# A decode step of cached attention plus a token mixer: mixer matmuls moved out of the last head, denominators before values, and more of the last V summed directly by [d, head]

## The chip, the cores and the metric

The kernel runs on one core of a Trainium2 chip. The metric is the device time of one execution, in microseconds (us), as the median of several executions. A profiled execution also gives a trace; its span is some 2 us shorter than the time (1274.7 against 1276.45 for the kernel before). Between traces, only durations and differences inside the span are compared.

In the profile, PE is TensorE's matmuls, PEld its weight loads, DVE is VectorE, ACT is ScalarE, and SP is the queue that issues the loads. The granted clock is the share of its full clock that the trace shows for TensorE; "half clock" is a stretch at 0.50. In a chain of waits, "issue" is time in which the engine waited for nothing that the profile shows.

## The reference

One query token attends over a cache of 65536 keys and values for 8 key-value heads (16 query heads, so 2 share each cache head; head size 256). K and V are 268 MB each in bf16. Beside it runs a small MLP ("mixer"), and a gate mixes both:

```
q = x @ wq                                  # 16 heads of 256
p = softmax(q . k * 256**-0.5)              # over 65536 positions
a = (p @ v) @ wo                            # 448 outputs
u = gelu(layernorm(x) outer w1 + b1)        # 448 x 1792
b = u @ w2 + b2                             # 448 outputs: "the mixer matmuls" do u @ w2
out = g * a + (1 - g) * b                   # g = sigmoid(x . gate_w)
```

## The kernel before

The cache comes in 32 rounds, 4 for each of 8 heads. A round is two K halves of 4 MB and one V buffer of 8 MB (128 tiles of 128 positions). For each round TensorE transposes K, makes the scores (`keys`), ScalarE takes exponentials into `pT`, and TensorE adds V into `acc` (`values`: two rows of 256, at four places of the partition axis, by `n % 4`) and the denominators through a matrix of ones. At a head's end `acc` is copied (`take`), turned into [d, head] by two products (`by_d`), divided by the denominators, and projected with `wo` (`project`).

The end of TensorE's program, and the `values` before (cuts marked):

```
pieces = [(0, 64), (64, 96), (96, 112), (112, 120), (120, 128)]   # the last V comes in five loads
NLATE = 112
...
def values(c0, n1=NV, last=False):
    for n in range(n1):
        r, nt = divmod(n, NT)
        if nt == 0 and r >= BODY - 2 and not last:
            pe.wait_ge(sem_exp, c0 + (r + 3))
        ...                                    # last: wait for the piece that n begins
        pe.matmul(acc[o:o + REP, 0:DH], pT[:, r, 2 * nt:2 * nt + 2], vbuf[:, n, :], ...)
    for r in range(BODY):                      # the 8 denominator matmuls
        ins = pe.matmul(acc[:, DENC:SELC], ones_sq[:, :], pT[:, r, :], ...)
    ins.then_inc(sem_pv, 1)                    # frees V; in the last round also starts `take`
...
# after the loop over heads and rounds:
pe.wait_ge(sem_exp, NC + 2)
pe.wait_ge(s_pb, FT)
for kt in range(FT):                           # FT = 14: the mixer matmuls
    ins = pe.matmul(sps[0:1, 1, 0:DM], w2p_b[:, kt:kt + 1], gu[:, kt, :], ...)
ins.then_inc(s_bmm, 1)
values(NC - BODY, n1=NLATE, last=True)
pe.wait_ge(s_cp, H)
by_d(sps[:, 0, 0:2 * REP], True)
for n in range(NLATE, NV):                     # tiles 112 to 127 straight by [d, head]
    ...
    for dj in range(2):
        ins = pe.matmul(sps[:, 0, dj * REP:(dj + 1) * REP], vbuf[:, n, dj:DH:2], pT[...], ...)
ins.then_inc(s_late, 1)
pe.wait_ge(sem_wo, 16 * H)
pe.wait_ge(s_oTn, H)
project()
```

The loads are issued in the order K half, K half, V. A K half is issued when the chunks of the half it replaces are transposed, a V when `sem_pv` says that the last one is used up. The "late tiles" are those that are summed directly by [d, head], two narrow matmuls for a tile, and need no copy behind them.

The softmax here doesn't subtract the row's maximum and nothing guards it: scores larger than these inputs give would overflow.

## Time and profile before

| | before |
|---|---|
| time, median of 3 | 1277.2 us (1276.92 to 1277.43) |
| load queue busy | 99.3% of 16 engines' span, 427 GB/s |
| TensorE / VectorE / ScalarE busy | 73% / 33% / 42% |
| end of the last key work | 1260.56 |
| last V piece landed | about 1267.3 |
| end of the last late tile | 1271.15 |
| end | 1274.7 |

First the page of the kernel before: part 3, the one large queue (packets, MB, share of the 16 DMA engines' span), and two lines of part 6 with the loads of the last V (size, us from issue to landing; the last line is the median of the last two pieces).

```profile
q1 hardware_dynamic: 16866, 544.22, 99.3%
...
vbuf<-in_A_v_cache_dram SPq DMA_DIRECT2D x1, 4096.0 KB, 23.6
...
vbuf<-in_A_v_cache_dram SPq DMA_DIRECT2D x2, 512.0 KB, 31.3
```

The loads never stop (99.3% of the 16 engines' span), so work taken out of the middle of the stream can save time only if the stream itself then gets faster. The five pieces were issued from 1233.79 to 1235.6; the last took 31.7 us and landed at about 1267.3.

Now the chain of waits, in order of time, at its end (start us, length us, what):

```profile
1258.96 1.59 PE sps L268 x64
1260.56 0.02 issue
1260.58 0.21 ACT pT L573
1260.79 0.52 issue
1261.31 3.65 PE sps L376 x12
...
1265.70 3.16 PE acc L292 x105
1268.86 0.31 PE acc L295 x8
...
1269.19 0.47 DVE accs L488
...
1269.70 0.64 PE sps L301 x4
1270.34 0.81 PE sps L388 x32
...
1271.48 0.93 PE prj L313 x4
```

L268 are the scores, L376 the mixer, L292 values, L295 denominators, L488 the copy, L301 `by_d`, L388 the late tiles, L313 the projection. There is no load in this stretch: after 1260.56 TensorE is never short of V, and its work ends the kernel. From the end of the key work to the end of the span it takes 14.1 us, and the mixer makes up about 4.4 of it.

### The profile page before, as it was taken

What the parts mean: (1) busy time and instruction counts of PE and PEld (TensorE: products, weight loads), DVE (VectorE), ACT (ScalarE), POOL (GpSimd) and SP (SyncE); (2) the same over time, 40 slices, a digit from 0 to 9 for tenths busy, and PEclk for the clock granted to TensorE, in tenths of its full rate; (3) what the DMA queues carried; (4) which work ended last, traced back from release to release, by engine and by line L of the source; (5) the groups of instructions that cost most, each with busy time, mean ns of one, the idle gap of its engine ahead of it and who ended that gap; (6) DMA issues with size and microseconds to landing.
All of it is one profiled execution on the core that took longest, in us unless ns stands there. A gap on an engine that the chain in (4) does not pass through costs nothing.

```text
span 1274.7 us, 37399 instructions
## 1 busy us (share of the span) xinstructions
PE 936.7 (73%) x16919; PEld 853.6 (67%) x16919; DVE 415.5 (33%) x727; ACT 534.9 (42%) x786; POOL 0.9 (0%) x7
## 2 busy tenths in 40 slices
PE   3878775878767687668876776866778667787768
PEld 3767765777657676567765676756677666777657
DVE  2786331333223332123331233312233222332223
ACT  1555433554324543335533345433455333553434
POOL 0000000000000000000000000000000000000000
PEclk9888888897778887788987789878889788898879
DMA  9999999999999999999999999999999999999996
GB/s 409 423 430 416 428 428 424 439 435 428 444 423 429 433 449 432 411 438 433 443 430 438 415 430 437 435 438 423 433 430 444 428 428 427 436 428 435 444 424 286
DMA packets 16892, 544.41 MB, mean 427 GB/s; under 512 B 1768, under 2 KB 3819, under 8 KB 4206
## 3 DMA queue, kind: packets, MB, share of 16 engines
q1 hardware_dynamic: 16866, 544.22, 99.3%
q8 instruction: 8, 0.13, 0.0%
q14 instruction: 6, 0.05, 0.0%
q10 hardware_dynamic: 12, 0.01, 0.0%
HBM read 544.22 MB, written 0.00 MB: 427 GB/s over the span
## 4 chain that ended last, share of the span: by engine, by line
DMA 75%; PE 20%; DVE 2%; issue 1%; ACT 1%; DVEq 0%; SPq 0%
DMA vbuf<-in_A_v_cache_dram 67%; PE acc L292 13%; DMA kring<-in_A_k_cache_dram 8%; PE kst L256 5%; PE sps L268 1%; PE acc L295 1%; ACT zring L569 0%; DVE ktT L483 0%; PE sps L376 0%; DVE zring L460 0%; DVE zring L464 0%; DVE wtmp L458 0%; DVE wtmp L454 0%; DVE uring L456 0%; PE prj L313 0%
## 5 line engine op out<-in xcount | busy, mean ns | idle before, releaser
L583 ACT ACTIVATE ktT<-kst 128x1024 bf16<-128x1024 bf16 x512 | 498.0, 1021 | 694.6 <-PE kst L256 694.3
L256 PE MATMUL kst<-ident,kring 128*128 128x128 f32 x4096 | 545.8, 293 | 125.3 <-DMA kring<-in_A_k_cache_dram 99.5
L483 DVE COPY ktT<-kst 128x1024 bf16<-128x1024 bf16 x512 | 352.8, 691 | 726.2 <-PE kst L256 703.8
L256 PEld LDWEIGHTS kst<-ident,kring 128*128 128x128 f32 x4096 | 494.5, 152 | 135.1 <-issue 115.8
L292 PE MATMUL acc<-vbuf,pT 128*2 128x256 bf16 x4080 | 179.3, 357 | 187.0 <-DMA vbuf<-in_A_v_cache_dram 186.2
L292 PEld LDWEIGHTS acc<-vbuf,pT 128*2 128x2 bf16 x4080 | 117.2, 108 | 242.1 <-DMA vbuf<-in_A_v_cache_dram 188.8
L268 PEld LDWEIGHTS sps<-qcur,ktT 128*128 128x128 bf16 x8192 | 238.4, 96 | 6.6 <-DVE ktT L483 3.7
L268 PE MATMUL sps<-qcur,ktT 128*128 128x2 bf16 x8192 | 237.5, 164 | 3.6 <-DVE ktT L483 3.5
L573 ACT ACTIVATE pT<-sps 128x32 bf16<-128x32 f32 x256 | 52.2, 204 | 13.4 <-PE sps L268 13.4
L488 DVE COPY accs<-acc 128x288 f32<-128x288 f32 x8 | 3.7, 458 | 98.1 <-PE acc L295 98.1
L295 PEld LDWEIGHTS acc<-pT,ones_sq 128*128 128x128 bf16 x256 | 8.5, 96 | 7.2 <-issue 7.2
L295 PE MATMUL acc<-pT,ones_sq 128*128 128x32 bf16 x256 | 11.7, 178 | 0.0
L313 PE MATMUL prj<-wo_sb,oTn 128*1 128x448 bf16 x32 | 9.1, 417 | 3.2 <-DVE oTn L499 3.2
L569 ACT ACTIVATE zring<-zring 128x448 bf16<-128x448 bf16 x14 | 8.1, 577 | 6.7 <-DVE zring L466 6.6
L330 PE MATMUL acc<-ones_sq,gu 1*128 1x1 bf16 x42 | 1.3, 161 | 8.4 <-DMA b_b<-in_B_b_dram 8.4
L330 PEld LDWEIGHTS acc<-ones_sq,gu 1*128 1x128 bf16 x42 | 1.2, 99 | 8.5 <-DMA b_b<-in_B_b_dram 8.5
L313 PEld LDWEIGHTS prj<-wo_sb,oTn 128*1 128x1 bf16 x32 | 2.4, 87 | 5.9 <-issue 4.6
L476 DVE TENSOR_TENSOR gu<-wtmp,zring 128x448 bf16<-128x448 bf16 x14 | 5.5, 392 | 1.1
L460 DVE TENSOR_TENSOR zring<-wtmp,uring 128x448 bf16<-128x448 bf16 x14 | 5.5, 392 | 1.0
L458 DVE TENSOR_TENSOR wtmp<-uring 128x448 bf16<-128x448 bf16 x14 | 5.5, 392 | 1.0
L464 DVE TENSOR_TENSOR zring<-uring,wtmp 128x448 bf16<-128x448 bf16 x14 | 5.5, 392 | 1.0
L306 PE MATMUL acc<-zrow,ones_sq 1*128 1x292 bf16 x8 | 2.5, 312 | 3.9 <-DVE accs L488 3.9
(79 smaller groups left out, 78.2 us busy)
## 6 DMA issues: line engine op xcount, KB each, us to landing
kring<-in_A_k_cache_dram SPq DMA_DIRECT2D x64, 4096.0 KB, 27.8
vbuf<-in_A_v_cache_dram SPq DMA_DIRECT2D x1, 4096.0 KB, 23.6
wo_sb<-in_A_wo_dram SPq DMA_DIRECT2D x8, 448.0 KB, 31.4
vbuf<-in_A_wq_dram SPq DMA_DIRECT2D x1, 3072.0 KB, 10.1
vbuf<-in_A_v_cache_dram SPq DMA_DIRECT2D x1, 2048.0 KB, 28.1
vbuf<-in_A_v_cache_dram SPq DMA_DIRECT2D x1, 1024.0 KB, 30.1
vbuf<-in_A_v_cache_dram SPq DMA_DIRECT2D x2, 512.0 KB, 31.3
vbuf<-in_A_wq_dram SPq DMA_DIRECT2D x1, 512.0 KB, 10.8
```

The lines of the kernel that those rows point to most:

```text
L256: ins = pe.transpose(kst[:, b, j * P:(j + 1) * P], kring_f[:, a, r * NT + 4 * b + j, :], ident[:, :])
L268: ins = pe.matmul(sps[:, par, 2 * nt:2 * nt + 2], ktT[:, par, b, ntl * DH + dj:(ntl + 1) * DH:2], qcur[:, dj, :], start=(dj == 0), stop=(d ...
L292: pe.matmul(acc[o:o + REP, 0:DH], pT[:, r, 2 * nt:2 * nt + 2], vbuf[:, n, :], start=False, stop=False, skip_group_check=True)
L295: ins = pe.matmul(acc[:, DENC:SELC], ones_sq[:, :], pT[:, r, :], start=False, stop=(r == BODY - 1), skip_group_check=True)
L313: ins = pe.matmul(prj[0:1, 0:DM], oTn[:, j:j + 1], wo_sb[:, hh, dj * DM:(dj + 1) * DM], start=False, stop=True, skip_group_check=True)
L458: vec.tensor_tensor(W, U, U, op=ALU.mult)
L460: vec.tensor_tensor(Z, W, U, op=ALU.mult)
L464: vec.tensor_tensor(Z, U, W, op=ALU.add)
L483: vec.tensor_copy(ktT[:, k % KTB, b, :], kst_b[:, b, :]).then_inc(sem_ev[b], 1)
L569: act.activation(zring[:, slot, :], zring[:, slot, :], AF.Tanh).then_inc(s_tanh, 1)
L573: act.activation(pT[:, k, :], sps[:, k % 2, 0:2 * NT], AF.Exp, scale=scale).then_inc(sem_exp, 1)
L583: act.activation(ktT[:, k % KTB, b, :], kst_b[:, b, :], AF.Copy).then_inc(sem_ev[b], 1)
```

## The change

The intent is to shorten this tail, the stretch from the end of the last scores on: the mixer goes to the end of head 6, where TensorE has time (in the next round it waits 7.26 us for V); denominators come before the values, while V is still on its way; and the last quarter of V (tiles 96 to 127, not 112 to 127) is summed directly by [d, head], so that the copy and `by_d` can run earlier and beside other tiles. The core of the diff, cut:

```
-    NLATE = 112
+    NLATE = 96
...
-            def values(c0, n1=NV, last=False):
+            def values(c0, u16, n1=NV, last=False):
+                for r in range(BODY):
+                    if r >= BODY - 2:
+                        pe.wait_ge(sem_exp, c0 + (r + 3))
+                    pe.matmul(acc[:, DENC:SELC], ones_sq[:, :], pT[:, r, :], ...)
                 for n in range(n1):
...
+                    elif n == 0:
+                        pe.wait_ge(sem_v, u16)
...
-                for r in range(BODY):
-                    ins = pe.matmul(acc[:, DENC:SELC], ones_sq[:, :], pT[:, r, :], ...)
                 ins.then_inc(sem_pv, 1)
...
+                with pe.If(g == H - 2):
+                    pe.wait_ge(s_pb, FT)
+                    for kt in range(FT):
+                        ins = pe.matmul(acc[0:1, 0:DM], w2p_b[:, kt:kt + 1], gu[:, kt, :], ...)
+                    ins.then_inc(s_bmm, 1)
+                    pe.wait_ge(s_brow, 1)          # VectorE has copied the row
+                    clear(acc[:, 0:NACC])
...
-            (the mixer matmuls)
-            values(NC - BODY, n1=NLATE, last=True)
+            values(NC - BODY, 16 * NP, n1=NLATE, last=True)
+            late_values(NLATE, pieces[3][0])       # tiles 96 to 111, beside the copy
             pe.wait_ge(s_cp, H)
-            by_d(sps[:, 0, 0:2 * REP], True)
-            for n in range(NLATE, NV): ...
+            by_d(sps[:, 0, 0:2 * REP])
+            late_values(pieces[3][0], NV).then_inc(s_late, 1)
```

VectorE's copy of the mixer's row moves in front of the last head's loop.

More of the change, by code (lines that the diff above doesn't have):

```diff
@@ L166, in bass_gated_mix__gqa_block_cached__mixer_token_mlp__decode_kernel @@
         s_late = new_sem("s_late")
+        s_brow = new_sem("s_brow")
         s_d2a = new_sem("s_d2a")
@@ L279, in keys @@
                 scores(BODY - 1, c0 + BODY - 1)
-            def values(c0, n1=NV, last=False):
+            def values(c0, u16, n1=NV, last=False):
+                for r in range(BODY):
+                    if r >= BODY - 2:
+                        pe.wait_ge(sem_exp, c0 + (r + 3))
+                    pe.matmul(acc[:, DENC:SELC], ones_sq[:, :], pT[:, r, :],
+                              start=False, stop=(r == BODY - 1), skip_group_check=True)
                 for n in range(n1):
                     r, nt = divmod(n, NT)
-                    if nt == 0 and r >= BODY - 2 and not last:
-                        pe.wait_ge(sem_exp, c0 + (r + 3))
@@ L287, in values @@
                     if last:
-                        for (n0, _), sem in zip(pieces, sem_vp):
-                            if n == n0:
-                                pe.wait_ge(sem, 16)
+                        piece_wait(n)
+                    elif n == 0:
+                        pe.wait_ge(sem_v, u16)
                     o = 32 * (n % 4)
-                    pe.matmul(acc[o:o + REP, 0:DH], pT[:, r, 2 * nt:2 * nt + 2], vbuf[:, n, :],
-                              start=False, stop=False, skip_group_check=True)
@@ L294, in values @@
-                for r in range(BODY):
-                    ins = pe.matmul(acc[:, DENC:SELC], ones_sq[:, :], pT[:, r, :],
-                                    start=False, stop=(r == BODY - 1), skip_group_check=True)
-                ins.then_inc(sem_pv, 1)
-            def by_d(dst, start):
+                    ins = pe.matmul(acc[o:o + REP, 0:DH], pT[:, r, 2 * nt:2 * nt + 2], vbuf[:, n, :],
+                                    start=False, stop=False, skip_group_check=True)
+                ins.then_inc(sem_pv, 1)
@@ new lines, in piece_wait, with late_values @@
+            def piece_wait(n):
+                for (n0, _), sem in zip(pieces, sem_vp):
+                    if n == n0:
+                        pe.wait_ge(sem, 16)
+            def late_values(n0, n1):
+                for n in range(n0, n1):
+                    r, nt = divmod(n, NT)
+                    piece_wait(n)
+                    for dj in range(2):
+                        ins = pe.matmul(sps[:, 0, dj * REP:(dj + 1) * REP], vbuf[:, n, dj:DH:2],
+                                        pT[:, r, 2 * nt:2 * nt + 2], start=(n == NLATE and dj == 0),
+                                        stop=(n == NV - 1), skip_group_check=True)
+                return ins
@@ L300, in by_d @@
+            def by_d(dst):
                 for dj in range(2):
                     ins = pe.matmul(dst[:, dj * REP:(dj + 1) * REP], accs[:, dj:DH:2], sel[:, :],
-                                    start=(start and dj == 0), stop=True, skip_group_check=True)
+                                    start=False, stop=True, skip_group_check=True)
                 return ins
@@ L362, in _ @@
                     with pe.If(j < NP - 1):
-                        pe.wait_ge(sem_v, u16)
-                        values(c0)
+                        values(c0, u16)
                 with pe.If(g < H - 1):
@@ L367, in _ @@
                     clear(acc[:, 0:NACC])
-                    by_d(acc[:, SELC:NACC], False).then_inc(s_sel, 1)
+                    by_d(acc[:, SELC:NACC]).then_inc(s_sel, 1)
                     pe.wait_ge(sem_wo, pe.snap(g * 16 + 16, min_val=16, max_val=16 * H))
@@ L371, in _ @@
                     project()
-            pe.wait_ge(sem_exp, NC + 2)
-            pe.wait_ge(s_pb, FT)
-            for kt in range(FT):
-                ins = pe.matmul(sps[0:1, 1, 0:DM], w2p_b[:, kt:kt + 1], gu[:, kt, :],
-                                start=(kt == 0), stop=(kt == FT - 1))
-            ins.then_inc(s_bmm, 1)
-            values(NC - BODY, n1=NLATE, last=True)
-            pe.wait_ge(s_cp, H)
-            by_d(sps[:, 0, 0:2 * REP], True)
-            for n in range(NLATE, NV):
-                r, nt = divmod(n, NT)
-                for (n0, _), sem in zip(pieces, sem_vp):
-                    if n == n0:
-                        pe.wait_ge(sem, 16)
-                for dj in range(2):
-                    ins = pe.matmul(sps[:, 0, dj * REP:(dj + 1) * REP], vbuf[:, n, dj:DH:2],
-                                    pT[:, r, 2 * nt:2 * nt + 2],
-                                    start=False, stop=(n == NV - 1), skip_group_check=True)
-            ins.then_inc(s_late, 1)
+                with pe.If(g == H - 2):
+                    pe.wait_ge(s_pb, FT)
+                    for kt in range(FT):
+                        ins = pe.matmul(acc[0:1, 0:DM], w2p_b[:, kt:kt + 1], gu[:, kt, :],
+                                        start=(kt == 0), stop=(kt == FT - 1))
+                    ins.then_inc(s_bmm, 1)
[3 more added lines that the diff above has]
+            late_values(NLATE, pieces[3][0])
+            pe.wait_ge(s_cp, H)
+            by_d(sps[:, 0, 0:2 * REP])
+            late_values(pieces[3][0], NV).then_inc(s_late, 1)
             pe.wait_ge(sem_wo, 16 * H)
@@ L532, in _ @@
                 finish_head(g)
-            with nc.Fori(NC - NCPH, NC, BODY, engines=on) as c0:
-                for k in range(BODY):
-                    evacuate(k, c0 + k)
             vec.wait_ge(s_bmm, 1)
-            vec.tensor_copy(brow1[:, :], sps[0:1, 1, 0:DM])
+            vec.tensor_copy(brow1[:, :], acc[0:1, 0:DM]).then_inc(s_brow, 1)
             vec.drain()
@@ L541, in _ @@
             vec.tensor_scalar(run[:, :], brow[:, :], stat[:, 6:7], None, op0=ALU.mult)
+            with nc.Fori(NC - NCPH, NC, BODY, engines=on) as c0:
+                for k in range(BODY):
+                    evacuate(k, c0 + k)
             take(NP)
```

## The prediction

> **What bounds it now.** The load stream. The page has the one data queue busy for 99.3% of 16 engines' span, at a mean of 427 GB/s; the stretch table shows 429 to 434 GB/s in every 100 us after the first. [...] 544 MB must come in, whatever the engines do. Queue waits show a load is always issued with at least one 4 MB K half still outstanding, so a release that comes a little earlier or later inside the stream should move nothing. Only what lies after the stream's end can be saved.
>
> **The tail before (chain of waits, order of time).** Last K lands at 1237.95; TensorE needs until 1260.6 for its keys; then 14 mixer matmuls, about 5 us (half clock, 0.37 us each); 112 values, about 3.5; denominators 0.31; copy of the sums 0.47; product by [d, head] 0.64; 16 late tiles 0.81; then to the end 3.55 us (normalise 0.17, projection 0.93, output 0.67, store). End 1274.7. The last V pieces (issue to landing) come at about 1257.4, 1262.3, 1264.7, 1266.0 and 1267.2. So TensorE, not the loads, ends the tail: its late tiles finish at 1271.15, about 4 us after the last piece.
>
> **What the change does.**
> - Mixer out of the tail: 5.3 us off this path. TensorE would get to the values at 1260.8.
> - Denominators first: 0.36 us (8 matmuls) before the values rather than after; in the tail also while V is still on its way. In the other 31 rounds V is released 0.3 us earlier; worth nothing under a full queue.
> - 96 instead of 112 tiles before the sums are copied; 32 late tiles as 64 narrow matmuls (before: 32 in 0.81 us, so about 1.6 us), half of them while the sums are copied.
> - New sum: denominators and 96 values end at about 1264.4; tiles 96 to 111 wait for their piece (1264.7) and end at about 1265.4; product by [d, head] until about 1266.1; tiles 112 to 119 until about 1266.6; the last piece lands at about 1267.2, its 16 matmuls 0.45 us: 1267.7 against 1271.15. Saving 3.4 us. The tail turns from TensorE-bound to load-bound, so about 2 of the 5.3 us are not gained.
> - Given back: [...] here one head's projection took 1.65 us, the last one 0.93. If it falls again, the last projection is up to 0.7 us longer; I count 0.3.
> - End of head 6: 14 mixer matmuls (5.2 us), copy 0.61, clear 0.3: TensorE some 6.4 us later into head 7. There it waits 7.26 us for V in that round (timeline, 1149.5), and an 8 MB V load is queued while it is late; absorbed, just.
>
> **Prediction.** 1277.2 - 3.2 = 1274.0 us; 8 in 10: 1272.4 to 1275.6. Faster by over 2%: 1%; within 2%: 98%; slower: 1%.
>
> **Signs.** Right: the chain's end shows a DMA wait on V before the last late tiles, no mixer; last late tile about 0.5 us after the last landing, within 1267 to 1268.5; V wait of head 7's first round shrunk from 7.3 to about 1 us, later rounds unchanged; load rate unchanged. Wrong: a gap in the loads at head 7's start; the last piece landing later than 1268.
>
> **What would make it wrong.** The stream ends at another time (0.2% of rate is 2.5 us, as much as the effect); head 7's delay not absorbed; a last landing nearer 1266.5 (gain 4); half clock through the whole tail (gain 2).

The sum comes to 1267.7 for the last late tile against 1271.15, so 3.45 us; less the 0.3 counted for half clock that is 3.2, and 1277.2 - 3.2 = 1274.0. Under "Given back", "it" in "if it falls again" is the granted clock (0.51 during the projection of 1.65 us, 1.00 during that of 0.93), and the 0.3 us are an estimate from these two projections, which lie 0.7 us apart.

## The result, and the profile after

The changed kernel took 1273.78 us (median of 4, 1271.96 to 1275.53) against 1277.29 (median of 4, 1276.92 to 1277.43). The ratio is 0.9973, with a 95% interval of 0.9956 to 0.999. It is the mean time of one kernel's fast runs over that of the other's of the same rounds, so not quite the ratio of the medians. By the limit of 2% it is "the same"; the saving is small, but clear of zero. Two more batches of five runs gave ratios of 0.9979 (0.9966 to 0.9993) and 0.9984 (0.997 to 0.9997). Over all 14 runs the mean saving against the runs of before in the same batch is (4 x 3.47 + 5 x 2.42 + 5 x 2.16) / 14 = 2.6 us.

The times of the changed kernel spread over 4.3 us (1271.96 to 1276.25), those of before over 2.7 in all batches (1275.25 to 1277.92), so the effect is no larger than the scatter of single runs.

The same parts of the page after, of the fastest of these runs:

```profile
q1 hardware_dynamic: 16866, 544.22, 99.6%
...
vbuf<-in_A_v_cache_dram SPq DMA_DIRECT2D x1, 4096.0 KB, 22.9
...
vbuf<-in_A_v_cache_dram SPq DMA_DIRECT2D x2, 512.0 KB, 30.6
```

The last piece was issued at 1235.1, took 31.0 us and landed at 1266.1. The rate of the stream did not change. This is the view of long windows (stretch, its length, busy time of PE, PEld, DVE, ACT and POOL, granted clock, DMA share, GB/s), before:

```profile
300.00:600.00 300.00, 224.76 (x4042) 205.99 (x4042) 90.83 (x138) 130.81 (x192) 0.00 (x0) 0.84 1.00 432
600.00:900.00 300.00, 221.01 (x3984) 201.43 (x3985) 86.56 (x132) 123.70 (x181) 0.00 (x0) 0.83 1.00 433
```

and after:

```profile
300.00:600.00 300.00, 225.62 (x4047) 208.29 (x4045) 90.81 (x138) 131.30 (x192) 0.00 (x0) 0.85 1.00 432
600.00:900.00 300.00, 222.58 (x3986) 202.04 (x3987) 86.67 (x132) 124.03 (x181) 0.00 (x0) 0.83 1.00 433
```

The last column says 432 and 433 GB/s in both. So the saving has to be sought in the tail. The end of the chain of waits after:

```profile
1258.82 1.58 PE sps L269 x64
1260.40 0.91 issue
1261.31 0.36 PE acc L287 x8
1261.67 2.72 PE acc L296 x96
1264.39 0.89 PE sps L310 x32
1265.27 0.47 PE sps L317 x4
1265.75 0.92 PE sps L310 x32
...
1266.99 0.93 PE prj L329 x4
```

L287 are the denominators, L296 the values, L310 the late tiles, L317 `by_d`. The key work ends where it did (1260.40 against 1260.56), and the span ends at 1270.2: 9.8 us later, not 14.1. The mixer is gone and the copy hides beside tiles 96 to 111. Two things are new: 0.91 us of "issue" before the denominators, and no wait for V on the chain, although the last piece landed (1266.1) just where TensorE came to its tiles (it ended them at 1266.66). The last 32 late matmuls took 0.92 us here and 0.81 in the trace before, so about 0.1 us of waiting for that piece may hide in them (an estimate). TensorE and the loads end the tail nearly together.

At the head's end where the mixer went, the timeline of TensorE before (start, us, engine, line, output and inputs, count, idle before and what ended it; the two windows differ, so the last count is cut by the window):

```profile
1118.76 1.65 PE L313 MATMUL prj<-wo_sb,oTn 128*1 128x448 bf16 x4 [0.42 <-DVE oTn L499]
...
1149.51 0.81 PE L292 MATMUL acc<-vbuf,pT 128*2 128x256 bf16 x12 [7.26 <-DMA vbuf<-in_A_v_cache_dram]
```

and after:

```profile
1116.60 0.92 PE L329 MATMUL prj<-wo_sb,oTn 128*1 128x448 bf16 x4 [0.41 <-DVE oTn L508]
1117.35 2.81 PE L390 MATMUL acc<-gu,w2p_b 128*1 128x448 bf16 x14
1120.87 0.29 PE L322 MATMUL acc<-zrow,ones_sq 1*128 1x292 bf16 x1 [0.71 <-DVE xcb_row L543]
...
1148.31 4.01 PE L296 MATMUL acc<-vbuf,pT 128*2 128x256 bf16 x72 [4.98 <-DMA vbuf<-in_A_v_cache_dram]
```

The mixer took 2.81 us here, at full clock (1.00), and the wait for V behind it fell only from 7.26 to 4.98 us.

### The profile page after: what moved, and what is told of

Same layout as the page of the kernel before. It is cut to its first block, busy times and chain, and to the rows that moved or that the text cites. A ratio compares the mean times of both kernels' runs of the same rounds, so it can differ in the third digit from the quotient of the medians.

```text
span 1270.2 us, 37440 instructions
## 1 busy us (share of the span) xinstructions
PE 944.5 (74%) x16936; PEld 861.9 (68%) x16936; DVE 415.7 (33%) x727; ACT 535.4 (42%) x786; POOL 0.9 (0%) x7
## 4 chain that ended last, share of the span: by engine, by line
DMA 73%; PE 21%; DVE 3%; issue 1%; ACT 1%; DVEq 0%; SPq 0%
DMA vbuf<-in_A_v_cache_dram 65%; PE acc L296 13%; DMA kring<-in_A_k_cache_dram 8%; PE kst L257 6%; PE sps L269 2%; ACT zring L578 0%; DVE ktT L492 0%; DVE wtmp L467 0%; DVE zring L469 0%; DVE zring L473 0%; DVE uring L465 0%; DVE wtmp L463 0%; DVE gu L485 0%; PE acc L390 0%; DVE wtmp L471 0%
## 5 line engine op out<-in xcount | busy, mean ns | idle before, releaser
L257 PE MATMUL kst<-ident,kring 128*128 128x128 f32 x4096 | 553.7, 296 | 128.6 <-DMA kring<-in_A_k_cache_dram 101.5
L257 PEld LDWEIGHTS kst<-ident,kring 128*128 128x128 f32 x4096 | 502.2, 153 | 141.1 <-issue 121.8
L296 PE MATMUL acc<-vbuf,pT 128*2 128x256 bf16 x4064 | 178.1, 357 | 168.1 <-DMA vbuf<-in_A_v_cache_dram 167.5
L296 PEld LDWEIGHTS acc<-vbuf,pT 128*2 128x2 bf16 x4064 | 116.5, 108 | 223.1 <-DMA vbuf<-in_A_v_cache_dram 170.2
L287 PE MATMUL acc<-pT,ones_sq 128*128 128x32 bf16 x256 | 16.4, 178 | 4.0 <-issue 0.9
L287 PEld LDWEIGHTS acc<-pT,ones_sq 128*128 128x128 bf16 x256 | 10.9, 96 | 7.2 <-ACT pT L582 6.2
```

The lines of the kernel that those rows point to most:

```text
L257: ins = pe.transpose(kst[:, b, j * P:(j + 1) * P], kring_f[:, a, r * NT + 4 * b + j, :], ident[:, :])
L287: pe.matmul(acc[:, DENC:SELC], ones_sq[:, :], pT[:, r, :], start=False, stop=(r == BODY - 1), skip_group_check=True)
L296: ins = pe.matmul(acc[o:o + REP, 0:DH], pT[:, r, 2 * nt:2 * nt + 2], vbuf[:, n, :], start=False, stop=False, skip_group_check=True)
```

## The experiments

Twelve runs were made in three batches of four; four of them repeat a kernel. Within a batch all were on one chip and shared nine runs of the kernel before (mean 1276.38, 1276.61 and 1276.60). Unless said otherwise there were five timed runs of each, and one of the executions was traced. "Below before" is the difference of the means within the batch. The tail is counted from the end of the last scores; the values are those of the timeline, which has them 0.07 us longer than the chain, as there they overlap with their neighbours.

| run | mean us | below before | key work end to span end, in the trace | mixer, values in the tail |
|---|---|---|---|---|
| first result (4 runs) | 1273.76 | 3.47 | 9.8 | -, 2.79 |
| after_again | 1273.96 | 2.42 | 11.2 | -, 4.25 |
| mixer_only | 1274.87 | 1.51 | 10.0 | -, 3.23 (112 tiles) |
| mixer_stays | 1275.99 | 0.39 | 13.0 | 2.81, 2.79 |
| dens_last | 1273.05 | 3.33 | 10.8 | -, 2.79 |
| before_again (one look) | | | 14.2 | 4.4, 3.2 (112 tiles) |
| mixer_x3 | 1274.34 | 2.27 | 11.8 | -, 4.46 |
| less_v | 1274.47 | 2.14 | 10.4 | -, 2.79 |
| peel | 1274.80 | 1.81 | 11.8 | -, 2.79 |
| after_third | 1274.43 | 2.16 | 9.9 | -, 2.79 |
| dens_last_2 | 1273.86 | 2.74 | 9.9 | -, 2.79 |
| peel_less_v | 1272.51 | 4.09 | 9.2 | -, 2.79 |
| peel_sums_first | 1275.63 | 0.97 | 12.3 | -, 2.96 |

The standard deviation of the five runs of one kernel was 0.6 to 1.4 us, so two means differ clearly only from about 1.5 us up. Where a trace shows the cause, the trace is used.

### Theories

Theory A: the saving is the shorter tail of TensorE alone. Theory B: part of it comes from the stream, as V is released 0.3 us earlier in 31 rounds (the first trace after had its "last K" land at 1236.74 rather than 1237.95). The "last K" of the prediction and the expectations is the last K that TensorE waits for, the first half of the last round; the second half landed at 1246.4 and 1247.6, before TensorE needed it.

**after_again.** The changed kernel, unaltered.

> The changed kernel once more, for a second trace and more times. Its first four times spread over 3.6 us (1271.96 to 1275.53), the kernel before only over 0.5. Theory A (the tail alone): from the end of the key work to the end of the kernel the trace shows 9.8 us again (14.1 before), and the spread comes from the end of the load stream: where a run is slow, the last V piece lands later than 1266 and the chain's end shows a DMA wait on V. Rival C (clock): the last piece lands as in the first trace, and slow runs have half clock in the tail. Mean expected 1273 to 1275.

The mean was 1273.96. The tail took 11.2 us, not 9.8, and the difference is in one line of the chain:

```profile
1261.43 0.92 issue
1262.34 0.36 PE acc L287 x8
1262.70 4.18 PE acc L296 x96
1266.88 0.91 PE sps L310 x32
```

The values took 4.18 us where they had taken 2.72; the granted clock was at half from 1263.75 to 1267.2. The last V piece landed at 1236.1 + 31.1 = 1267.2, before TensorE was ready for it. So theory A's account of the spread (late loads) did not hold for this execution, and rival C (clock) did. The last piece landed 1.1 us later than in the first trace, too, and the key work ended 1.0 us later (1261.43 against 1260.40; 1262.14 in after_third): the part before the tail has a scatter of its own.

**mixer_only.** The kernel before, with only the mixer moved.

```
-            (the mixer matmuls in the tail)
+                with pe.If(g == H - 2):
+                    (the mixer matmuls, into acc; wait for VectorE's copy; clear acc)
```

> The kernel before, with only the mixer matmuls moved to the end of head 6; denominators stay last, 112 tiles go into the sums. Theory A: most of the gain is here, 2.5 to 4 us below the kernel before, as the 5.3 us of mixer leave the tail and up to 1 us comes back as a wait for V. Theory B (the stream: earlier release of V in all 31 rounds shifts its end): only about 3 us or less, with the last V piece landing at 1266 or later; the rest of the gain needs the denominators first.

It was 1.5 us below before, less than theory A said, with an interval of the ratio that just includes 1 (0.9976 to 1.0003). By its times it leaves room for theory B. Its trace has a tail of 10.0 us, nearly the 9.8 of the whole change, both without half clock before the end: by the traces (one of each kernel) the move of the mixer alone takes 4.1 of the 4.3 us that the first two differ by. What the other two parts of the change add is thus 0.2 us by the traces and 0.9 us by the means of this batch (standard error about 0.7), and is not settled.

**mixer_stays.** The changed kernel, with the mixer left in the tail.

```
-                with pe.If(g == H - 2): (the mixer)
+            (the mixer in front of the last values)
```

> The changed kernel, but the mixer matmuls stay in the tail as before. Theory A: TensorE-bound tail as before, within 1 us of the kernel before (0 to 1 us faster). Theory B: 1 us or more faster, since V is released earlier and the stream ends earlier, and last K lands at about 1236.7 and not 1238.

It was 0.4 us below before, as theory A said and theory B did not: the earlier release of V, which this kernel has in full, buys nothing that these times can tell from zero. Theory B's other sign, the landing of the last K, did appear (1236.6), and in dens_last too (1237.8). But the unaltered changed kernel had it at 1236.7, 1238.0 and 1238.5 in its three traces, so the sign is scatter and decides nothing. This trace also shows what the mixer costs without half clock:

```profile
1260.40 0.56 issue
1260.96 2.81 PE sps L390 x14
1263.77 0.30 PE acc L287 x8
```

It took 2.81 us here, and 4.4 in the trace before, where the clock was at half. In this trace half clock fell on the projection instead (1.64 us, not 0.93).

**dens_last and dens_last_2.** The changed kernel, with the denominators behind the values again (and the wait for the exponentials moved to the values).

```
-                for r in range(BODY): (wait for the exponential; denominator matmul)
                 for n in range(n1): ...
+                for r in range(BODY): (denominator matmul)
                 ins.then_inc(sem_pv, 1)
```

> The changed kernel, but the denominator matmuls come after the values in every round, as before. Theory A: within 0.5 us of the changed kernel: the 0.36 us of the denominators only change places. Theory B: about 1 us slower than the changed kernel, with the last K landing about 1 us later.

> The changed kernel with the denominators after the values, again: it was 0.9 us faster than the changed kernel last time, on five runs each that spread over 2.3 us. If the order does nothing, it is within 0.7 us of the changed kernel of this batch, on either side; if denominators first cost something, it is again 0.7 us or more faster.

The means were 0.91 and 0.57 us below those of the changed kernel in the same batches. Theory B expected dens_last to be slower than the changed kernel, and falls. Whether the order costs some tenths of a us is not settled: over both batches it is 0.74 us, with a standard error of about 0.4 (ten runs each). In the first of these traces the tail ended on the loads (a wait of 0.59 us for the last piece, at 1267.1), in the second the chain runs on TensorE, though the last piece landed (1267.3) just as its matmuls began.

**before_again.** The kernel before.

> The kernel before, a second trace. In its first trace the granted clock fell to half just while the mixer ran in the tail (14 matmuls, about 5.2 us), in the run with the mixer left in the tail it stayed full (2.81 us). Theory D (the half clock falls on the tail at random): the mixer takes either about 2.8 or up to 5.2 us here, and if 2.8, the tail from the end of the key work to the end is about 12 us instead of 14.1. Rival: the mixer always takes 5 us in this kernel.

The mixer was at half clock again: its twelve plain matmuls took 3.72 us, with the clock at half from 1262.7 to 1266.1, and the tail 14.2 us. So theory D is not supported by this trace: of two executions of the kernel before, both had half clock in the mixer. That half clock belongs to the mixer in the tail as such is not so either, as mixer_stays shows.

**mixer_x3.** The changed kernel, with the mixer matmuls at the end of head 6 done three times.

```
-                    for kt in range(FT):
+                    for kt in list(range(FT)) * 3:
```

> The changed kernel with the mixer matmuls at the end of head 6 done three times (42 instead of 14, same result): 5.6 us more TensorE work there at full clock. Theory A (that place has slack): within 1 us of the changed kernel, the wait for V in the next round falls from 5 us towards zero, and the load rate stays. Rival: the delay holds up later loads, and the stream ends 2 us or more later.

It was 2.27 us below before, as good as the unaltered kernel (2.42 and 2.16 in the other batches). The timeline at the head's end:

```profile
1119.35 8.11 PE L390 MATMUL acc<-gu,w2p_b 128*1 128x448 bf16 x42
1128.16 0.29 PE L322 MATMUL acc<-zrow,ones_sq 1*128 1x292 bf16 x1 [0.71 <-DVE xcb_row L543]
1150.02 0.62 PE L287 MATMUL acc<-pT,ones_sq 128*128 128x32 bf16 x8
1150.56 1.70 PE L296 MATMUL acc<-vbuf,pT 128*2 128x256 bf16 x56
```

The mixer took 8.11 us and the wait for V is gone, so TensorE was late for V in that round, and still nothing came of it: in the four slices of its page that span 1081 to 1209 us the DMA share is 90% or more and the rate 431 to 443 GB/s, so the next loads were queued in time. The end of head 6 is a free place for all 42 matmuls.

**less_v.** The changed kernel, with 2 MB less of the last V. The result is wrong (32 tiles are left over from the round before); the comparison with the reference says little about a few tiles of 65536 positions.

```
-                        eng.dma_start(vbuf[:, n0:n1, :]..., v_src(j, n0, n1))
+                        nl = n1 - 32 if n0 == 0 else n1
+                        eng.dma_start(vbuf[:, n0:nl, :]..., v_src(j, n0, nl))
```

> The changed kernel, but the first piece of the last V load brings only half its tiles (2 MB less; wrong result on purpose), so that the stream ends some 4.9 us earlier. Theory A1 (the tail of the changed kernel is bound by TensorE, not by loads): within 0.6 us of the changed kernel, and the trace has no wait for V in the tail. Theory A2 (bound by loads, as I predicted: last landing to last late tile): 1.5 to 4 us faster.

The last piece landed at 1236.5 + 26.0 = 1262.5, and the kernel was 2.1 us below before, not faster than the changed kernel. Its chain begins the tail as the changed kernel does, without a wait for V, though here the projection ran at half clock (1.67 us):

```profile
1261.79 0.92 issue
1262.71 0.36 PE acc L288 x8
1263.07 2.72 PE acc L297 x96
```

So the loads alone do not bind the changed kernel (A1).

**peel.** The changed kernel, with TensorE's last round, and the mixer, as straight code behind the loops.

```
-            with nc.Fori(0, H, ...) as g:
-                with nc.Fori(0, PPH, ...) as m: keys; with pe.If(j < NP - 1): values
-                with pe.If(g < H - 1): (head's end)
-                with pe.If(g == H - 2): (mixer)
+            with nc.Fori(0, H - 1, ...) as g:
+                with nc.Fori(0, PPH, ...) as m: keys; values
+                (head's end)
+            (mixer)
+            with nc.Fori(NP - PPH, NP - 1, ...) as j: keys; values
+            keys(NC - BODY, 16 * NP)
```

> The changed kernel with TensorE's last round (and the mixer) taken out of the loop as straight code. In the trace of the changed kernel TensorE sits 0.9 us between the last scores and the first denominators, though six of the eight need no wait. Theory E (this gap is leaving the loops and branches): the gap falls to about 0.3 us (the last exponential), the kernel is 0.3 to 0.7 us faster as long as TensorE binds. Rival: the gap is the last exponential's semaphore: nothing changes.

The gap of 0.91 us is gone, as theory E said: the trace has no idle time of TensorE between scores and denominators. But the kernel was not faster than the changed one (1.8 us below before). Its timeline shows where the gain went:

```profile
1259.67 1.74 PE L269 MATMUL sps<-qcur,ktT 128*128 128x2 bf16 x64
1261.28 0.62 PE L287 MATMUL acc<-pT,ones_sq 128*128 128x32 bf16 x8
1261.82 2.79 PE L296 MATMUL acc<-vbuf,pT 128*2 128x256 bf16 x96
1265.74 0.35 PE L310 MATMUL sps<-pT,vbuf 128*128 128x2 bf16 x8 [1.13 <-DMA vbuf<-in_A_v_cache_dram]
...
1267.07 0.99 PE L317 MATMUL sps<-sel,accs 128*128 128x2 f32 x4
...
1269.27 1.65 PE L329 MATMUL prj<-wo_sb,oTn 128*1 128x448 bf16 x4 [0.35 <-DVE oTn L510]
```

TensorE now waits 1.13 us for the piece of tiles 96 to 111, and, with half clock from 1266.9 on, `by_d` (0.99 for 0.61) and the projection (1.65 for 0.92) are longer.

**peel_less_v.** Straight code and 2 MB less of V (wrong).

```
(the edits of peel and of less_v together)
```

> TensorE's last round as straight code and 2 MB less of the last V (wrong result on purpose). Straight code alone gained nothing (1275.1), less V alone gained nothing (1275.0). Theory G (the two limits lie within 1 us of each other, so each hides what the other would give): both together are 1 us or more below either, 1273 or less, with no wait for V in the tail. Rival (straight code has no value at all): 1274 to 1275 again.

It was 4.09 us below before, at 1272.51: 2.3 us below straight code alone and 2.0 below less V alone (each against the before of its own batch). The trace has no wait for V in the tail:

```profile
1261.76 2.79 PE L297 MATMUL acc<-vbuf,pT 128*2 128x256 bf16 x96
1264.48 0.95 PE L311 MATMUL sps<-pT,vbuf 128*128 128x2 bf16 x32
```

This is what theory G said: in the changed kernel TensorE and the loads end so close together that taking away either limit alone shows nothing. The traces of the changed kernel say the same without these experiments. The 16 matmuls of the last piece take 0.57 us (dens_last). Landing and matmuls add up to 1266.7 in the first trace and 1268.4 in after_third, and the last tile ended at 1266.66 and 1268.45; in after_again, with half clock, it ended 1.3 us behind that sum. Not all of the gain is accounted for, though: the tail of peel_less_v is 0.7 us shorter than that of after_third, and the means of the two differ by 1.9. And a rival for peel alone remains, that straight code itself delays the loads (see peel_sums_first).

**after_third.** The changed kernel once more.

> The changed kernel a third time, beside the others of this batch. Mean 1273 to 1275 again. Theory F (half clock): the traces so far show the clock fall to half for 3.4 us in the tail in those executions in which some 1.8 us or more of the last scores and the gap behind them fell into the 3.4 us just before; then values take 4.2 to 4.5 us and not 2.7. This trace should show either both or neither. Rival: it falls regardless of what came before.

It was 2.16 us below before. The trace had neither: of the last scores and the gap, 1.79 us fell into the 3.4 us window before (in each trace the clock changed at multiples of 3.4 us, see the next section), and the values ran at full clock (2.79 us). This agrees with theory F, but dens_last_2 in the same batch does not: 2.1 us fell into its window, and the clock stayed full; so it did in dens_last, with 1.9. In the three other traces with half clock in the tail's values or mixer (before, before_again, mixer_x3) it was 2.35 to 2.5 us, and in after_again 2.0. So theory F is a tendency in these traces, not a rule that is shown.

**peel_sums_first.** Meant to be better than both: straight code, and `by_d` before the wait for tiles 96 to 111.

```
-            late_values(NLATE, pieces[3][0])
             pe.wait_ge(s_cp, H)
-            by_d(sps[:, 0, 0:2 * REP])
-            late_values(pieces[3][0], NV).then_inc(s_late, 1)
+            by_d(sps[:, 0, 0:2 * REP], start=True)
+            late_values(NLATE, NV).then_inc(s_late, 1)
```

> A version meant to be better: straight code for the last round, and the product by [d, head] of the 96 summed tiles is made before the wait for the piece of tiles 96 to 111, not behind it. In the trace with straight code TensorE waited 1.1 us for that piece and did the product (0.85 us at half clock) only then. Theory G: 0.8 us or more below straight code alone, about 1273.5, last late tile within 0.7 us of the last landing. Rival: nothing gained, as half clock takes it back.

It was only 0.97 us below before: worse, if anything. In its trace the last piece landed at 1237.2 + 32.1 = 1269.3, the latest of all; TensorE waited three times for V (0.43, 0.28 and 0.65 us), did its last tiles 0.6 us after the landing, as meant, and then projected at half clock (1.65 us). In all three kernels with straight code the last V was issued at 1234.65 to 1235.40, against 1233.05 to 1235.04 in the others. The record hints at a delay by straight code: the first K half of the last round landed at 1238.85 to 1239.3 in these three traces and at 1236.6 to 1238.5 in the eleven others, and the last V of the two with full V landed latest of all (1268.1 in peel). So peel may have gained nothing in part because its loads came later; that was not tested. No version that beats the changed kernel with a right result came out of this.

## Why the prediction was right or wrong

The number was right: 1274.0 predicted, 1273.78 measured, in the range, and "within 2%". The mechanism, a shorter tail, was right too; that the number fits so closely is partly luck. The traced execution, the fastest of its four, ended its late tiles at 1266.66 and not at 1267.7, so its tail saved a us more than predicted, while the mean of all 14 runs saved 2.6 us and not 3.2. Point by point:

- **The bound.** "Only what lies after the stream's end can be saved": right for the parts of this change. The rate is the same in both long windows (432 and 433 GB/s); that it could not be higher was not shown. And mixer_stays and dens_last show no gain from the earlier release of V. But the chain that ends the kernel leaves the loads earlier than "the stream's end" says: in the first trace after, TensorE waited 3.6 us for the first K half of the last round (landed at 1236.74), and the trace names no wait for a load from then on. The 23.5 us of key work behind it, the first of them at half clock (until 1242.5), lie on that chain too, while V still streams beside it. I took that K half for the last K; what a shorter key work would save was not tried.
- **The sum of the tail.** Right up to the end of the values, but two terms were off and cancelled, by luck. I let TensorE begin its denominators at 1260.8; it began at 1261.31, since leaving the loops costs 0.91 us (0.92 in after_again and less_v) where I had read the gap before as the wait for the exponential (peel shows it: the gap goes with the loops). In return, the 96 values took 2.72 us, where my sum had about 3.2 for them. They ended at 1264.39, and I had said 1264.4.
- **"Mixer out of the tail: 5.3 us."** Mis-sized. The chain before has 4.4 us of it (1261.31 to 1265.70; it began at full clock), and the gap in front stays. And 1.6 us of that belong to the clock, not to the work: at full clock the 14 matmuls take 2.81 us (mixer_stays), while both traces of before had most of them at half clock. I sized the removed work as 14 times the half-clock duration.
- **"The tail turns from TensorE-bound to load-bound."** Half wrong. I put the last landing at 1267.2; in the first trace after it was 1266.1, and less_v shows that TensorE still binds: less V, no gain. The last late tile did end 0.56 us after the landing, as predicted, but the chain has no wait for V there. In truth both limits lie close together: within some 0.1 us in two traces of the changed kernel and 1.3 us in the third, and peel_less_v, where both were moved, was clearly faster. Which one ends the chain can change with the execution: the two traces of one kernel, dens_last and dens_last_2, differ in it.
- **"Given back: half clock, I count 0.3."** Right in kind; too small as a worst case. The projection took 0.93 us in the three traces after, but the values took 4.18 instead of 2.72 in one of them. Half clock (1.4 us) and the scatter of the part before the tail (last landing at 1266.1, 1267.2 and 1267.8, end of the key work at 1260.40, 1261.43 and 1262.14) account for the differences between the three traces of the changed kernel; the runs without a trace are not explained by that.
- **"TensorE some 6.4 us later into head 7; absorbed, just. V wait about 1 us."** Absorbed: right. Just: wrong. The wait fell only to 4.98 us, as the mixer ran at full clock (2.81, not 5.2 us) and the projection before it too (0.92, not 1.65), although the denominators, now in front of the wait, take 0.6 us of it. Three times the mixer was absorbed as well.

Open: why half clock falls on some tails and not on others; whether denominators first cost some tenths; whether straight code delays the stream, and how much of peel's missing gain that is.

On the granted clock the traces show this: in the last 50 us of every trace it changed at multiples of 3.4 us with one phase (a last change behind the end of the work left out), in the trace before at 1262.15, 1265.55 and 1272.4, and the phase differed from execution to execution. That idle time of TensorE lowers it, on which "given back" rested, was not shown. In the trace before it fell to half at 1262.15, though TensorE had idled only 0.76 us in the 3.4 us before (which also held 1.6 us of scores with 2 columns and the beginning of the mixer with 1 output row). In less_v it fell at 1267.95 though the trace has TensorE busy for all of the 3.4 us before, with values, late tiles and `by_d`. And it stayed full after windows with idle gaps of 0.91 us (the first trace after) and 1.0 us (mixer_only). So idle time alone does not decide it here.

## What to carry to other kernels

Here 14 matmuls went from the tail of a load-bound kernel into a place where their engine waited 7.26 us for loads, and the whole change saved 2.6 us. A tail of TensorE that was shortened further gained nothing by itself (peel: TensorE then waited 1.13 us for a load), as the loads were close to being the limit too: in two traces of three the last landing with its matmuls and TensorE's last tile ended within some 0.1 us of each other. So compute both ends (last landing, last matmul) before promising more. When two limits end that close together, an experiment that removes one may show nothing, so remove both: less V was 2.14 us below before and straight code 1.81, where the changed kernel was at 2.42 and 2.16, and both together were at 4.09. And size a removed TensorE stretch at both clocks: the same 14 matmuls took 2.8 us at full clock and 4.4 us where most of them were at half clock.
